# Linear attention with a gated projection on one core: 128-token states, stacked scores, log sums on the matrix engine

## The chip, the cores and the metric

The kernel runs on one core of a Trainium2 chip. A core has five engines that run side by side, each through its own list of instructions: TensorE (PE, matrix products into the PSUM memory), VectorE (DVE), ScalarE (ACT), GpSimd (POOL) and SyncE (SP, which here only issues DMA transfers). The metric is the device time of one launch in microseconds (us).

## The reference

```python
f = 1.0 / (1.0 + np.exp(-f_logit))
state = np.zeros((B, H, D, D))
for t in range(S):
    state = f[:, :, t, :, None] * state + np.einsum('bhd,bhe->bhde', k[:, :, t], v[:, :, t])
    y[:, :, t] = np.einsum('bhd,bhde->bhe', q[:, :, t], state)
x = y.transpose(0, 2, 1, 3).reshape(B, S, H * D)
gate = sigmoid(causal_conv(x, conv_w))        # 5 taps, per channel
out = (gate * (x @ w_val)) @ w_out
```

B = 4, H = 8, S = 768, D = 48, so H * D = 384. Everything is float32. Three weights come as float64 and are turned into float32 on the chip.

## The kernel before, in words

Tokens are cut into NC = 6 chunks of C = 128; each is worked as two halves of HC = 64 tokens. Two heads (s = 0, 1) are stacked on the partitions, at rows 0 and 64, so B * H = 32 heads are BP = 16 pairs; `h` = 0, 1 names a half of the pairs (HP = 8). The recurrence is taken in chunks. For chunk c:

- `pexp`, `pln` (ACT) make log(1 + exp(-f_logit)); `scan` (DVE) sums it along the tokens of a chunk; `exp2` and `exp1` (ACT) make e to the plus and minus that sum; `pmulk`, `pmulq` (DVE) multiply k and q by them.
- `scores` (PE) multiplies k and q inside each half of 64 tokens; `mask` (DVE) copies the product from PSUM to `asb` with the causal triangle `tri`.
- `ktrans` (PE) turns k over, `kevac` (ACT) copies it to `ksb`, `dstate` (PE) makes what each half of 64 tokens adds to the state: u = 0 for the first half, u = 1 for the second. `stmid` (DVE) adds the first to get `mid`, the state in the middle of the chunk, `stend` (DVE) adds the second, and `stmul` (POOL) multiplies by the chunk's whole decay. There is thus a state for each 64 tokens.
- `apply` (PE) sums into x: q on the state (`st` for the first half, `mid` for the second) and `asb` on v. In n = 0 the matmuls use tiles of 64 rows by 32 columns of the array, in n = 1 tiles of 128 by 32.
- `xevac` (ACT) copies x to `xf`. Then the projection of chunk n: `msplit`, `mlow` split x into two float32r parts, `mval` and `mout` are the two products (9 matmuls of 512 columns for each third m of the 384 channels), the convolution is either `conv` (PE, chunks 0, 1, and 5 in two halves named 5 and 6) or `mlast` and `mconv` (ACT and DVE, chunks 2 to 4), then `gate`, `mmul`, `mhigh`, `mrest`, `mstore` and `out`.

The order of all this is the string `PROGRAM`: pieces written out by hand, one after another. `Ordered.call` (line 114, which is the line of nearly every row of the profile) ties each instruction of PE, DVE and ACT to the one before it on its engine, so each engine runs its pieces strictly in that order. `busy n` puts n matmuls on zeros in front of the next piece that takes a PSUM buffer. PSUM has three buffers `pair` and two `mps`: a piece that takes a `pair` waits until the last reader of that buffer is done.

A float32 matmul that is written once is two matmuls in the trace (a half of `scores` is 32 written and 64 in the trace); a transpose is one.

Of the kernel before, what the change touches and what calls it, by code (L numbers as in the profile page):

```python
# [48 lines left out]
loadf 0 0; pexp 0 0; pln 0 0; scan 0 0; loadf 0 1; pexp 0 2; loadk 0 1; wload 0; weight 0; weight 0; weight 0; weight  # L49
0; weight 0; weight 0; pln 0 2; scan 0 2; pexp 0 1; pln 0 1; scan 0 1; loadk 0 2; exp2 0 2; pmulk 0 2; busy 44; ktrans  # L50
0 1; exp1 0 2; loadq 0 2; pmulq 0 2; busy 1; scores 0 1; wload 1; weight 1; weight 1; weight 1; exp2 0 1; pmulk 0 1;
weight 1; mask 0 1; weight 1; exp2 0 0; exp1 0 1; kevac 0 1; exp1 0 0; loadv 0 2; busy 2; dstate 0 1; stmid 0 1; busy
3; apply 0 1 0; apply 0 1 1; loadf 1 0; pexp 1 0; pln 1 0; weight 1; weight 1; weight 1; weight 0; weight 2; halo 0;
stend 0 1; stmul 0 1; loadk 0 0; loadv 0 1; loadq 0 0; pmulk 0 0; loadq 0 1; pmulq 0 0; pmulq 0 1; okc 0; busy 2;
scores 0 0; ktrans 0 0; kevac 0 0; loadv 1 1; scan 1 1; exp2 1 1; exp1 1 1; weight 3; scan 1 0; exp2 1 0; exp1 1 0;
loadk 1 1; loadv 0 0; loadq 1 0; dstate 0 0; stmid 0 0; mask 0 0; apply 0 0 0; apply 0 0 1; stend 0 0; loadk 1 0;
pmulk 1 1; ktrans 1 1; weight 2; weight 3; xevac 0 1; kevac 1 1; loadq 2 1; loadq 1 1; pmulk 1 0; ktrans 1 0; kevac 1
0; dstate 1 1; weight 3; pmulq 1 0; scores 1 0; xevac 0 0; msplit 0; stmul 0 0; loadf 2 0; pexp 2 0; pln 2 0; weight
2; pmulq 1 1; mask 1 0; weight 3; weight 2; busy 1; scores 1 1; mask 1 1; weight 2; stmid 1 1; weight 2; weight 2;
stend 1 1; weight 3; okc 1; conv 0; gate 0 0; gate 0 1; gate 0 2; scan 2 1; loadv 1 0; dstate 1 0; stmid 1 0; scan 2  # L60
0; apply 1 1 0; apply 1 1 1; apply 1 0 0; apply 1 0 1; stend 1 0; weight 3; exp2 2 1; loadk 2 1; wload 2; pmulk 2 1;
ktrans 2 1; stmul 1 1; weight 2; weight 4; weight 4; weight 4; exp1 2 1; exp2 2 0; halo 1; xevac 1 1; stmul 1 0; pmulq
2 1; scores 2 1; weight 3; weight 3; weight 5; kevac 2 1; loadv 2 1; dstate 2 1; loadq 2 0; weight 4; mlow 0; mval 0
0; mval 0 1; mask 2 1; loadk 2 0; pmulk 2 0; ktrans 2 0; xevac 1 0; weight 4; stmid 2 1; apply 2 1 0; mmul 0 0; exp1 2
0; okc 2; pmulq 2 0; stend 2 1; weight 4; loadq 3 1; weight 5; loadk 3 1; loadf 3 0; pexp 3 0; pln 3 0; scan 3 1;
scores 2 0; kevac 2 0; loadv 2 0; dstate 2 0; stmid 2 0; mask 2 0; weight 4; weight 4; weight 6; stend 2 0; weight 5;
weight 6; weight 6; exp2 3 1; pmulk 3 1; weight 6; mval 0 2; exp1 3 1; msplit 1; weight 5; weight 6; weight 5; apply 2
0 0; apply 2 0 1; halo 2; ktrans 3 1; kevac 3 1; xevac 2 0; mmul 0 2; weight 5; weight 6; apply 2 1 1; xevac 2 1; conv
1; mlow 1; pmulq 3 1; mhigh 0 0; mmul 0 1; mrest 0 0; mhigh 0 2; weight 6; weight 5; scan 3 0; loadv 3 0; loadv 3 1;
scores 3 1; mask 3 1; stmul 2 1; dstate 3 1; stmid 3 1; loadk 4 0; stmul 2 0; loadf 4 0; pexp 4 0; pln 4 0; mhigh 0 1;  # L70
mrest 0 2; mrest 0 1; stend 3 1; mval 1 0; apply 3 1 0; gate 1 0; mmul 1 0; mlast 2 0; scan 4 0; mconv 2 0 0; apply 3
1 1; gate 1 1; gate 1 2; exp2 3 0; exp1 3 0; loadk 3 0; pmulk 3 0; loadv 4 0; loadq 3 0; loadk 4 1; loadk 5 1; loadq 4
0; mconv 2 0 1; pmulq 3 0; weight 6; halo 3; weight 5; mout 0 0; mstore 0 0; mout 0 2; mstore 0 2; loadq 5 1; out 0 0;
out 0 2; ktrans 3 0; kevac 3 0; exp2 4 0; mout 0 1; scan 4 1; mhigh 1 0; mrest 1 0; pmulk 4 0; loadv 5 1; mstore 0 1;
out 0 1; exp2 4 1; exp1 4 1; mlast 2 1; dstate 3 0; stmid 3 0; scores 3 0; mask 3 0; mval 1 2; mval 1 1; okc 3; mmul 1
2; mlast 2 2; mhigh 1 2; apply 3 0 0; apply 3 0 1; stend 3 0; mconv 2 1 0; mmul 1 1; mhigh 1 1; mconv 2 0 2; mrest 1
2; mrest 1 1; mout 1 2; msplit 2; xevac 3 1; exp1 4 0; mstore 1 2; xevac 3 0; stmul 3 1; mout 1 1; mstore 1 1; stmul 3
0; loadk 5 0; loadf 5 0; pexp 5 0; out 1 2; mout 1 0; mstore 1 0; out 1 1; loadv 4 1; out 1 0; ktrans 4 0; kevac 4 0;
mconv 2 1 1; pmulk 4 1; ktrans 4 1; mconv 2 1 2; mconv 2 2 0; mconv 2 1 3; pmulq 4 0; scores 4 0; mconv 2 2 1; mconv 2
0 3; mlow 2; mconv 2 2 2; dstate 4 0; mask 4 0; mconv 2 2 3; stmid 4 0; pln 5 0; scan 5 0; mval 2 0; gate 2 0; mmul 2  # L80
0; mval 2 1; gate 2 1; mmul 2 1; scan 5 1; apply 4 0 0; mval 2 2; gate 2 2; mmul 2 2; mhigh 2 1; mrest 2 1; mhigh 2 0;
mrest 2 0; apply 4 0 1; loadv 5 0; kevac 4 1; dstate 4 1; mhigh 2 2; exp2 5 1; exp1 5 1; mrest 2 2; mout 2 0; mstore 2
0; mlast 3 2; mlast 3 0; stend 4 0; loadq 4 1; pmulq 4 1; scores 4 1; mout 2 2; mstore 2 2; pmulk 5 1; stmid 4 1; okc
4; mask 4 1; apply 4 1 0; apply 4 1 1; pmulq 5 1; stend 4 1; mconv 3 0 0; mconv 3 2 0; msplit 3; out 2 0; mconv 3 2 1;
mlow 3; mlast 3 1; mconv 3 1 0; mconv 3 0 1; mconv 3 1 1; mconv 3 0 2; mconv 3 0 3; mconv 3 2 2; ktrans 5 1; kevac 5
1; halo 4; xevac 4 1; mout 2 1; mstore 2 1; mval 3 1; exp2 5 0; exp1 5 0; gate 3 0; xevac 4 0; stmul 4 0; stmul 4 1;
dstate 5 1; stmid 5 1; scores 5 1; mask 5 1; mconv 3 2 3; gate 3 2; mconv 3 1 2; mconv 3 1 3; gate 3 1; mval 3 0; mmul
3 0; mhigh 3 0; apply 5 1 0; apply 5 1 1; halo 5; xevac 5 1; mlast 4 1; loadq 5 0; out 2 2; pmulq 5 0; pmulk 5 0; okc
5; msplit 6; mval 3 2; mmul 3 2; mhigh 3 2; scores 5 0; mmul 3 1; mrest 3 0; mask 5 0; ktrans 5 0; kevac 5 0; mhigh 3
1; conv 6; gate 6 0; mlast 4 2; dstate 5 0; mrest 3 2; mrest 3 1; mout 3 0; mstore 3 0; gate 6 1; gate 6 2; out 2 1;  # L90
mlow 6; stmid 5 0; mval 6 0; mmul 6 0; mconv 4 1 0; mconv 4 1 1; mout 3 2; mhigh 6 0; mrest 6 0; mlast 4 0; mconv 4 0
0; out 3 0; mout 3 1; mstore 3 2; out 3 2; mval 6 2; mstore 3 1; out 3 1; mconv 4 0 1; mconv 4 0 2; mconv 4 1 2; mmul
6 2; mhigh 6 2; msplit 4; mconv 4 0 3; mconv 4 2 0; mrest 6 2; mval 6 1; mmul 6 1; mhigh 6 1; apply 5 0 0; apply 5 0
1; mconv 4 2 1; xevac 5 0; mrest 6 1; mout 6 2; gate 4 0; mstore 6 2; msplit 5; out 6 2; mout 6 0; mstore 6 0; out 6
0; mout 6 1; mstore 6 1; out 6 1; mconv 4 1 3; mlow 4; mval 4 1; mval 4 0; mlow 5; check 0; mval 5 0; mconv 4 2 2;
mmul 4 0; gate 4 1; mmul 4 1; mhigh 4 1; mconv 4 2 3; gate 4 2; mval 5 2; mval 4 2; mmul 4 2; mrest 4 1; mhigh 4 0;
mrest 4 0; mhigh 4 2; mrest 4 2; conv 5; gate 5 0; mmul 5 0; gate 5 1; gate 5 2; mval 5 1; mmul 5 1; mhigh 5 1; mout 4
0; mhigh 5 0; mrest 5 0; mmul 5 2; mrest 5 1; mout 4 2; mstore 4 0; out 4 0; mhigh 5 2; mrest 5 2; mstore 4 2; out 4
# [683 lines left out]
```

## Time and profile before

| what | value |
|---|---|
| median of 3 runs | 231.31 us (230.03, 231.31, 234.48) |
| the profiled execution, its own time | 233.41 us |
| its span in the profile | 231.2 us, so 2.2 us lie around it |
| ScalarE, GpSimd busy | 137.3 us (59%), 42.2 us (18%) |
| weight loads of TensorE busy | 146.0 us (63%) |
| read from and written to HBM | 29.11 MB and 4.72 MB |
| largest loads | `v` 640 KB in 8.7 us, `k` 512 KB in 4.9 us, `q` 512 KB in 6.7 us from issue to landing |

Busy shares are averages over stages with different limits: the first 40 us load at over 370 GB/s, the second half hardly loads. PE counts a matmul as busy while it is in the pipeline, so several overlap. "issue" as the releaser of a wait is time for which the profile shows nothing that the engine waited for.

### The profile page before, as it was taken

What the parts mean: (1) busy time and instruction counts of PE and PEld (TensorE: products, weight loads), DVE (VectorE), ACT (ScalarE), POOL (GpSimd) and SP (SyncE); (2) the same over time, 40 slices, a digit from 0 to 9 for tenths busy, and PEclk for the clock granted to TensorE, in tenths of its full rate; (3) what the DMA queues carried; (4) which work ended last, traced back from release to release, by engine and by line L of the source; (5) the groups of instructions that cost most, each with busy time, mean ns of one, the idle gap of its engine ahead of it and who ended that gap; (6) DMA issues with size and microseconds to landing.
All of it is one profiled execution on the core that took longest, in us unless ns stands there. A gap on an engine that the chain in (4) does not pass through costs nothing.

```text
span 231.2 us, 10393 instructions
## 1 busy us (share of the span) xinstructions
PE 190.3 (82%) x4805; PEld 146.0 (63%) x4809; DVE 165.4 (72%) x204; ACT 137.3 (59%) x198; POOL 42.2 (18%) x52
## 2 busy tenths in 40 slices
...
PEclk9999755575999599979999999999999999999997
...
GB/s 204 371 415 416 421 417 109 239 240 96 6 188 382 118 3 96 234 264 100 94 209 162 110 366 125 3 4 96 45 7 3 3 50 94 48 23 3 45 136 34
DMA packets 10129, 34.56 MB, mean 149 GB/s; under 512 B 1248, under 2 KB 2016, under 8 KB 9184
## 3 DMA queue, kind: packets, MB, share of 16 engines
...
q8 instruction: 39, 0.64, 1.1%
...
HBM read 29.11 MB, written 4.72 MB: 146 GB/s over the span
## 4 chain that ended last, share of the span: by engine, by line
PE 66%; issue 13%; DVE 9%; DMA 5%; ACT 3%; SPq 1%; POOL 0%; DVEq 0%; ACTq 0%; POOLq 0%
PE pair L114 43%; PE mps L114 23%; DMA rawcw<-in_cw 2%; DMA out<-osb 2%; DVE asb L114 2%; DVE pre L114 1%; ACT e L114 1%; DVE e L114 1%; DVE qb L114 1%; DVE mid L114 1%; DVE kb L114 1%; DVE xL L114 1%; ACT ksb L114 1%; DVE rg L114 1%; SPq L648 1%
## 5 line engine op out<-in xcount | busy, mean ns | idle before, releaser
L114 ACT ACTIVATE e<-e 112x1024 f32<-112x1024 f32 (+2 forms) x42 | 48.9, 1179 | 6.1 <-DMA e<-in_f 3.8
L114 PE MATMUL pair<-asb,vb 128*32 128x64 f32 (+1 forms) x1152 | 29.1, 235 | 10.5 <-issue 10.5
L114 DVE TENSOR_TENSOR_SCAN e<-keep,e 112x1024 f32<-112x1024 bf16 (+1 forms) x13 | 29.8, 2301 | 0.3 <-ACT e L114 0.2
L114 PEld LDWEIGHTS pair<-asb,vb 128*32 128x32 f32 (+1 forms) x1152 | 22.6, 117 | 11.3 <-issue 11.3
L366 POOL TENSOR_TENSOR st<-st,e 112x512 f32<-112x512 f32 x10 | 17.1, 1709 | 64.6 <-DVE st L114 37.6
L114 ACT COPY ksb<-pair 128x864 f32<-128x864 f32 x12 | 10.6, 881 | 28.9 <-PE pair L114 28.7
L114 DVE SCALAR_TENSOR_TENSOR pre<-xf,cws,pre 128x512 f32<-128x512 f32 x36 | 26.6, 764 | 0.2
L114 DVE TENSOR_TENSOR asb<-pair,tri 128x1024 f32<-128x1024 f32 x12 | 14.7, 1221 | 15.6 <-PE pair L114 12.7
L114 PE MATMUL pair<-qb,kb 48*64 48x64 f32 x768 | 16.2, 231 | 9.8 <-issue 9.6
L114 PE MATMUL mps<-rg,woH 128*128 128x512 f32 x72 | 23.3, 404 | 0.0
L114 PEld LDWEIGHTS pair<-qb,kb 48*64 48x64 f32 x768 | 14.0, 144 | 13.2 <-issue 12.4
L114 PE MATMUL pair<-qb,mid 48*32 48x64 f32 (+1 forms) x576 | 17.9, 231 | 3.1 <-DVE asb L114 2.0
L114 PE MATMUL pair<-xf,WD 32*32 32x512 f32 (+1 forms) x280 | 19.7, 633 | 0.0
L114 PE MATMUL mps<-xf,WD 32*32 32x256 f32 (+1 forms) x200 | 19.7, 555 | 0.0
L114 PE MATMUL pair<-vb,ksb 64*48 64x64 f32 x704 | 16.5, 243 | 3.2 <-ACT ksb L114 1.9
L114 PEld LDWEIGHTS pair<-vb,ksb 64*48 64x48 f32 x704 | 14.4, 140 | 6.4 <-ACT ksb L114 2.4
L114 DVE TENSOR_TENSOR kb<-kb,e 112x1024 f32<-112x1024 f32 (+1 forms) x13 | 18.3, 1416 | 0.0
L114 PE MATMUL pair<-idle 128*128 128x512 bf16 x49 | 14.7, 455 | 4.2 <-DVE pair L114 3.7
L114 PE MATMUL mps<-xH,wvH 128*128 128x512 f32 x39 | 17.0, 436 | 0.0
L114 PE MATMUL mps<-xL,wvH 128*128 128x512 f32 x39 | 16.2, 416 | 0.3 <-DVE xL L114 0.3
L114 PE MATMUL mps<-xH,wvL 128*128 128x512 f32 x39 | 16.0, 409 | 0.0
L114 DVE TENSOR_TENSOR qb<-qb,e 112x1024 f32<-112x1024 f32 (+1 forms) x13 | 15.8, 1222 | 0.0
(108 smaller groups left out, 380.9 us busy)
## 6 DMA issues: line engine op xcount, KB each, us to landing
...
```

The lines of the kernel that those rows point to most:

```text
L114: ins = emit(*a, **kw)
L366: nc.gpsimd.tensor_tensor(out=s, in0=s, in1=E1[c % NB][:112, HS[h], C - 1 : C].to_broadcast([112, HP, HC]), op=ALU.mult)
L648: nc.sync.dma_start(dst[: src.shape[1]], src[c, :, x0:x1])
```

## The change

**One state per 128 tokens.** `dstate` contracts over all 128 tokens at once, from a second layout of v (`vs`, loaded by the new `loadw`, 512 KB for each half of a chunk's pairs). `stmid` and `mid` are gone, `stend` of chunk 0 takes the decay along with it, and the last chunk makes neither `ktrans` nor `dstate`.

**Scores.** They are made for one batch b of four pairs at a time. Of the four quarters of a 128 by 128 block three are made: the first 64 keys against all 128 queries (a matmul of 128 columns) and the last 64 keys against the last 64 queries. `mask` copies the two triangles, the new `cross` (ACT) the full quarter. `asb` has three buffers in place of two.

**Apply.** n = 0 is now the state alone (tiles of 64 by 32, then 112 by 32), n = 1 the scores alone (64 by 32, then 128 by 32); the first matmuls of each have 128 columns.

**Log sums.** For chunks 0 and 1 f comes with the tokens on the partitions (`ft`), and `csum` (PE) sums with one matmul for each pair against the triangle `below`; `exp1` and `exp2` read the sum from PSUM. The scans of these two chunks are gone.

**Order.** `PROGRAM` is written anew from beginning to end.

```diff
+CUM = (0, 1)
...
+    def csum(c, x0, x1):
+        t = pair("c", c, x0)[:].rearrange("p a t -> p (a t)")
+        for i in range(x1 - x0):
+            PE.matmul(t[:112, i * C : i * C + C], logs(c, x0, x1)[:, i], below[:], start=True, stop=True)
...
     def ktrans(c, h):
+        t = pair("k", c, h)[:].rearrange("p a t -> p (a t)")
+        for i in range(HP):
+            PE.transpose(t[:, i * C : i * C + 112], kb[c % NB][:112, h * HP + i], ident[:112, :112])
...
     def dstate(c, h):
+            for s in range(2):
+                PE.matmul(t[rows(s), 0, i * HC : i * HC + HC], ks[:, i, s], vs[:, h * HP + i, s * HC : s * HC + HC],
+                          start=True, stop=True, tile_position=(0, s * HC))
...
+    def scores(c, b):
+        t, qt, kt = pair("s", c, b), qb[c % NB], kb[c % NB]
+        for p in range(NP):
             for u in range(2):
                 for s in range(2):
+                    at = HC * (s ^ u)
+                    PE.matmul(t[at : at + HC, u, p * C : p * C + C - u * HC], kt[rows(s), b * NP + p, u * HC : u * HC + HC],
+                              qt[rows(s), b * NP + p, u * HC :], start=True, stop=True, tile_position=(s * 64, at))
...
+    def mask(c, b):
+        DVE.tensor_tensor(out=ASB[aslot(c, b)][:, :, 0:HC],
+                          in0=held["s", c, b][:].rearrange("p u (a t) -> p (u a) t", t=C)[:, :, 0:HC],
+                          in1=tri[:].unsqueeze(1).to_broadcast([C, 2 * NP, HC]), op=ALU.mult)
+    def cross(c, b):
+        ACT.copy(ASB[aslot(c, b)][:, 0:NP, HC:], held["s", c, b][:, 0].rearrange("p (a t) -> p a t", t=C)[:, :, HC:])
+        done("s", c, b)
...
     def apply(c, h, n):
+        for b in range(2):
+            for z in range(NP):
+                bp = (2 * h + b) * NP + z
+                for s in range(2):
+                    if n == 0:
+                        lhs, rhs = st[rows(s), bp, 32:64], qt[rows(s), bp]
+                    else:
+                        r = slice(s * HC, s * HC + HC)
+                        lhs, rhs = vt[r, bp, 32:64], ASB[aslot(c, 2 * h + b)][r, z]
...
+                if n == 0:
+                    ops = [(1, 0, st[:, bp, 0:32], qt[:112, bp])]
+                else:
+                    ops = [(1, 0, vt[:, bp, 0:32], at_[:, z])]
+                    ops += [(g, 1, vt[:, bp, VA + at : VA + at + 32], at_[:, NP + z, 0:HC]) for g, at in ((0, 32), (1, 0), (2, 64))]
...
+        "loadw": lambda c, h: load(vs[:, HS[h]], vn, c, h * HP, h * HP + HP),
```

Three places of the new order. The first is PE at the start, before. The rows stand behind the 44 matmuls on zeros (`idle`): the transposes of k (`kb`) for pairs 8 to 15 of chunk 0 come next, then the scores of q (`qb`) and k. Each row says what is written, what is read, and the shape written, with the count of equal ones.

```order
L114 MATMUL pair_100<-idle 128x512
L114 MATMUL pair_100<-ident,kb_66 128x48 x18
L114 LDWEIGHTS idle
L114 MATMUL pair_101<-idle 128x512
L114 MATMUL pair_101<-qb_64,kb_66 64x64 x32
```

The same place after the change (`below` is the triangle, `e_81` the logarithms of f). The sum of pairs 0 to 3 stands directly behind the 44, then come four matmuls on zeros, and the rows begin at the last of these.

```order
L119 MATMUL pair_102<-idle 128x512
L119 MATMUL pair_102<-below,e_81 112x128 x4
L119 MATMUL pair_103<-below,e_81 112x128 x8
L119 LDWEIGHTS idle
L119 MATMUL pair_101<-idle 128x512
L119 MATMUL pair_101<-ident,kb_66 128x112 x8
```

Before, the transposes are the first real work behind the 44; now the sums of all three parts of chunk 0 stand between, and the transposes wait for what is made from the sums.

The second place is PE in the apply of one half of the pairs, before (chunk 2; `st` and `mid` are the states, `asb` the masked scores, `vb` is v).

```order
L114 MATMUL pair_100<-qb_64,st_73 32x64 x8
L114 MATMUL pair_100<-qb_64,mid 32x64 x8
L114 MATMUL pair_100<-asb_84,vb_68 32x64 x8
L114 MATMUL pair_100<-qb_64,st_73 32x64 x8
L114 MATMUL pair_100<-qb_64,mid 32x64 x8
L114 MATMUL pair_100<-asb_84,vb_68 32x64 x8
L114 MATMUL pair_100<-qb_64,st_73 32x64 x4
L114 MATMUL pair_100<-qb_64,mid 32x64 x4
L114 MATMUL pair_100<-asb_84,vb_68 32x64 x16
L114 MATMUL pair_100<-qb_64,st_73 32x64 x4
L114 MATMUL pair_100<-qb_64,mid 32x64 x4
L114 MATMUL pair_100<-asb_84,vb_68 32x64 x16
```

The apply of one half after the change (chunk 1, second half; the transposes of chunk 2 stand in its middle).

```order
L119 MATMUL pair_101<-qb_65,st_75 32x128 x24
L119 MATMUL pair_102<-ident,kb_66 128x112 x8
L119 MATMUL pair_101<-asb_84,vb_69 32x128 x8
L119 MATMUL pair_101<-asb_85,vb_69 32x128 x8
L119 MATMUL pair_101<-asb_84,vb_69 32x128 x4
L119 MATMUL pair_101<-asb_84,vb_69 32x64 x12
L119 MATMUL pair_101<-asb_85,vb_69 32x128 x4
L119 MATMUL pair_101<-asb_85,vb_69 32x64 x12
```

96 written matmuls of 64 columns are now 72, of which 48 have 128 columns.

The third place is ACT, before, from the first copy of turned k (`ksb`) to the second; `e_81`, `e_82` and `e_83` hold the sums and their exponentials, `work` and `wvH` are weights.

```order
L114 COPY ksb_87<-pair_100 128x864
L114 ACTIVATE e_81<-e_81 112x512
L114 ACTIVATE e_82,sums<-e_82 112x2048
L114 ACTIVATE e_82<-e_82 112x2048
L114 CAST wvH<-work 128x384
L114 COPY ksb_86<-pair_102 128x864
```

The same stretch after the change.

```order
L119 COPY ksb_87<-pair_101 128x768
L119 ACTIVATE e_82<-e_82 128x1792
L119 COPY asb_85<-pair_102 128x4x64
L119 ACTIVATE e_83<-pair_103 112x1024
L119 ACTIVATE e_81<-pair_103 112x1024
L119 COPY asb_84<-pair_101 128x4x64
L119 ACTIVATE work<-work 128x384
L119 ACTIVATE e_83<-pair_102 112x1024
L119 COPY ksb_88<-pair_103 128x768
```

The copies of the full quarter (`asb<-pair`) now stand between long exponentials, and the `pair` buffer of the scores comes free only when its copy is done.

More of the change, by code (lines that the diff above doesn't have):

```diff
@@ L48 @@
 PROGRAM = """
[L49 to L98, printed above, removed]
@@ L99 @@
-2; mout 5 0; mout 5 1; mstore 5 0; out 5 0; mstore 5 1; out 5 1; mout 4 1; mstore 4 1; out 4 1; mout 5 2; mstore 5 2;
-check 1; check 2; out 5 2
+loadf 0 0; halo 0; pexp 0 0; pln 0 0; busy 44; csum 0 0; loadf 0 1; pexp 0 1; pexp 0 2; pln 0 1; busy 4; csum 0 1; pln
+0 2; csum 0 2; exp2 0 0; exp2 0 1; exp1 0 0; loadq 0 1; loadk 0 1; pmulk 0 1; loadq 0 0; loadk 0 0; pmulk 0 0; busy 1;
+ktrans 0 0; exp1 0 1; pmulq 0 1; wload 0; weight 0; weight 0; weight 0; weight 0; pmulq 0 0; busy 3; scores 0 1;
@@ new lines @@
+weight 0; mask 0 1; weight 0; weight 0; loadf 1 0; pexp 1 0; loadk 0 2; loadw 0 0; kevac 0 0; dstate 0 0; stend 0 0;
+scores 0 0; mask 0 0; pln 1 0; cross 0 1; csum 1 0; exp2 0 2; exp1 0 2; wload 1; pmulk 0 2; ktrans 0 1; cross 0 0;
+csum 1 1; okc 0; loadq 0 2; pmulq 0 2; weight 1; weight 1; weight 1; weight 1; weight 1; weight 1; exp2 1 0; loadv 0
+0; kevac 0 1; loadw 0 1; dstate 0 1; exp1 1 0; loadv 0 1; apply 0 0 1; stend 0 1; scores 0 3; exp2 1 1; exp1 1 1;
+loadk 1 0; pmulk 1 0; ktrans 1 0; weight 1; xevac 0 0; scores 0 2; kevac 1 0; loadk 1 1; pmulk 1 1; ktrans 1 1; weight
@@ new lines @@
+2; mask 0 3; cross 0 3; loadq 1 0; pmulq 1 0; busy 2; scores 1 0; weight 2; weight 2; weight 1; weight 3; weight 3;
+kevac 1 1; apply 1 0 0; mask 0 2; cross 0 2; scores 1 1; mask 1 0; cross 1 0; loadf 2 0; pexp 2 0; loadv 0 2; apply 0
+1 1; xevac 0 1; weight 2; weight 3; okc 1; weight 2; weight 3; weight 2; weight 3; mask 1 1; cross 1 1; loadq 1 1;
+pmulq 1 1; pln 2 0; weight 3; weight 2; loadw 1 0; dstate 1 0; stend 1 0; scores 1 2; mask 1 2; cross 1 2; msplit 0;
+scan 2 0; exp2 2 0; exp1 2 0; loadw 1 1; dstate 1 1; stend 1 1; scores 1 3; loadv 1 0; apply 1 0 1; halo 1; xevac 1 0;
@@ new lines @@
+conv 0; apply 1 1 0; scan 2 1; exp2 2 1; mask 1 3; weight 3; cross 1 3; mlow 0; wload 2; loadk 2 0; loadk 2 1; pmulk 2
+1; ktrans 2 1; loadv 1 1; apply 1 1 1; weight 2; weight 4; stmul 1 1; stmul 1 0; weight 3; mval 0 1; weight 5; weight
+4; weight 4; exp1 2 1; okc 2; weight 4; gate 0 0; kevac 2 1; weight 4; weight 4; weight 4; pmulk 2 0; ktrans 2 0;
+loadq 2 0; pmulq 2 0; gate 0 1; loadw 2 1; dstate 2 1; weight 5; weight 5; weight 5; gate 0 2; xevac 1 1; mmul 0 1;
+weight 5; scores 2 1; kevac 2 0; stend 2 1; weight 4; weight 6; weight 6; scores 2 0; mask 2 1; weight 5; weight 6;
@@ new lines @@
+mask 2 0; weight 6; loadf 3 0; pexp 3 0; pln 3 0; loadw 2 0; dstate 2 0; stend 2 0; weight 6; weight 6; cross 2 1;
+cross 2 0; mhigh 0 1; weight 5; mval 0 2; apply 2 0 0; loadq 2 1; pmulq 2 1; mval 0 0; msplit 1; scan 3 0; exp2 3 0;
+scores 2 3; mmul 0 0; scores 2 2; mask 2 2; cross 2 2; loadq 3 1; weight 6; scan 3 1; mhigh 0 0; halo 2; stmul 2 1;
+loadv 2 0; loadk 3 0; loadv 2 1; apply 2 0 1; mask 2 3; xevac 2 0; loadw 3 1; stmul 2 0; loadf 4 0; pexp 4 0; cross 2
+3; pmulk 3 0; mrest 0 0; mrest 0 1; mmul 0 2; mlow 1; pln 4 0; scan 4 0; loadk 4 0; loadk 3 1; exp2 3 1; pmulk 3 1;
@@ new lines @@
+conv 1; apply 2 1 0; ktrans 3 0; kevac 3 0; apply 2 1 1; mval 1 1; loadk 4 1; loadq 3 0; loadw 3 0; dstate 3 0; gate 1
+0; gate 1 1; mmul 1 1; ktrans 3 1; mhigh 0 2; mrest 0 2; xevac 2 1; weight 5; weight 6; halo 3; gate 1 2; scan 4 1;
+mval 1 2; mmul 1 2; exp1 3 1; pmulq 3 1; mlast 2 0; mconv 2 0 0; exp1 3 0; mout 0 2; mstore 0 2; exp2 4 0; mout 0 0;
+mstore 0 0; kevac 3 1; pmulq 3 0; pmulk 4 0; mout 0 1; mhigh 1 2; loadv 4 1; loadq 4 1; loadq 4 0; loadv 4 0; out 0 2;
+dstate 3 1; scores 3 2; stend 3 0; mconv 2 0 1; scores 3 3; stend 3 1; stmul 3 1; mstore 0 1; mhigh 1 1; mask 3 2;
@@ new lines @@
+2 2 3; pmulq 4 0; pln 5 0; scan 5 1; kevac 4 0; gate 2 0; gate 2 1; pmulq 4 1; scan 5 0; mval 2 1; mmul 2 1; apply 3 1
+0; ktrans 4 1; loadw 4 1; out 1 2; loadv 3 1; apply 3 1 1; scores 4 1; kevac 4 1; dstate 4 1; xevac 3 1; gate 2 2;
+mhigh 2 1; mlast 3 2; mask 4 1; dstate 4 0; stend 4 0; stend 4 1; mval 2 2; mmul 2 0; mhigh 2 0; okc 4; mmul 2 2;
+cross 4 1; scores 4 0; mask 4 0; cross 4 0; scores 4 2; scores 4 3; mconv 3 2 0; mrest 2 1; mhigh 2 2; mrest 2 2;
+mrest 2 0; out 1 1; loadv 5 1; loadq 5 0; exp2 5 0; exp1 5 0; apply 4 0 0; apply 4 0 1; halo 4; xevac 4 0; mout 2 1;
@@ L305, in gla_moe @@
     rows = lambda s: slice(s * 64, s * 64 + D)
-    held, spare, free, uses = {}, list(pairs), list(mps), [8 * NC + sum(n < NC - 1 for n in CONV)]
+    held, spare, free, uses = {}, list(pairs), list(mps), [10 * NC - 4 + sum(n < NC - 1 for n in CONV) + sum(2 if c else 3 for c in CUM)]
     def pair(*key):
```

215 lines of the change are left out of this document (99 added, 116 removed).

## The prediction

> **What bounds the kernel now.** I read the page first, then busy time by stage, then the chain of waits in a stretch where TensorE (PE) is much idle, then PE's waits and single rows.
>
> ```profile
> span 231.2 us, 10393 instructions
> PE 190.3 (82%) x4805; PEld 146.0 (63%) x4809; DVE 165.4 (72%) x204; ACT 137.3 (59%) x198; POOL 42.2 (18%) x52
> PEclk9999755575999599979999999999999999999997
> ...
> q8 instruction: 39, 0.64, 1.1%
> ```
>
> PE is the busiest, but its granted clock falls to about half in slices 5 to 10 and again in slice 14. The q8 row is the fetching of instructions: 39 packets with 0.64 MB, about 16 KB each. PE's 4805 matmuls and 4809 weight loads are most of the program's instructions, so about 256 of them, or 128 matmuls with their loads, come in one packet.
>
> The stages, cut at the first transposes (16.09 us), at the end of the second convolution on PE (108.43) and at PE's last product; after the stretch, each engine's busy time and count, the granted clock, and the DMA share with GB/s:
>
> ```profile
> 0.00:16.09 16.09, 12.44 (x45) 4.97 (x46) 12.67 (x16) 9.78 (x17) 7.12 (x27) 1.00 0.84 325
> 16.09:108.43 92.34, 66.84 (x2227) 50.06 (x2233) 64.32 (x72) 49.55 (x63) 28.41 (x19) 0.80 0.58 214
> 108.43:224.90 116.47, 110.97 (x2539) 91.00 (x2539) 88.22 (x116) 78.01 (x120) 6.68 (x6) 1.00 0.23 79
> 224.90:231.20 6.30, 0.00 (x0) 0.00 (x0) 0.15 (x1) 0.00 (x0) 0.00 (x0) 0.74 0.19 61
> ```
>
> So the middle stage is bound by no engine (PE 66.84 of 92.34 at clock 0.80), and the late one by PE (110.97 of 116.47). What holds the middle stage is seen in the chain (start, length, what), and in PE's waits of that stage and of the whole run (total, times, longest):
>
> ```profile
> 59.06 1.85 PE pair L114 x118
> 60.91 0.42 issue
> 61.33 2.16 PE pair L114 x128
> 63.49 1.16 issue
> 64.65 1.82 PE pair L114 x103
> 66.47 1.91 issue
> 68.38 2.64 PE pair L114 x126
> 71.02 3.96 issue
> 74.98 2.41 PE pair L114 x43
> ```
> ```profile
> PE pair L114 <- issue: 22.1, 13, 4.0
> ...
> PE pair L114 <- issue: 24.0, 15, 4.0
> PE pair L114 <- ACT ksb L114: 1.9, 2, 1.0
> ```
>
> PE stops after 128 matmuls (61.33), again after about 128, each time for nothing that another engine does. **PE waits for its own instructions**: 22.1 us in 13 waits in the middle stage, 1.9 in the late one.
>
> **The change part by part: how many matmuls.** Scores stay at 64 written for a chunk. The apply goes from 192 to 144 (chunk 0 from 144 to 96), `dstate` from 64 to 32, the transposes from 36 to 16; chunk 5 loses `dstate` (32) and transposes; `csum` adds 32 in all, zeros 5. Float32 counts double, so apply -576, `dstate` -384, transposes -136, `csum` +64, zeros +5: 4805 becomes 3778. From the first transposes to the point where the second convolution and the apply of chunk 2 are done, I count 1696 against the stage's 2227. Both orders reach this point with the same work behind them, but for some of the projection.
>
> **What one matmul costs.**
>
> ```profile
> 159.47 0.35 PE L114 MATMUL pair<-qb,st 48*32 48x64 f32 x16
> ...
> 159.93 0.22 PE L114 MATMUL pair<-asb,vb 64*32 64x64 f32 x1
> 160.29 0.34 PE L114 MATMUL pair<-asb,vb 64*32 64x64 f32 x12
> 160.57 0.32 PE L114 MATMUL pair<-qb,st 112*32 112x64 f32 x8
> 160.81 0.63 PE L114 MATMUL pair<-asb,vb 128*32 128x64 f32 x32
> 162.05 0.76 PE L114 MATMUL pair<-ident,kb 48*128 48x48 f32 x18
> ...
> 17.10 1.16 PE L114 MATMUL pair<-qb,kb 48*64 48x64 f32 x64 [0.25 <-DVE work L114]
> ...
> 18.73 1.11 PE L114 MATMUL pair<-vb,ksb 64*48 64x64 f32 x64
> ```
>
> A run of equal rows lasts one matmul's 0.22 us and the steps between starts: (0.63 - 0.22) / 31 = 13.2 ns in the apply (four tiles of 32 columns), (1.16 - 0.22) / 63 = 14.9 in the scores and (1.11 - 0.22) / 63 = 14.1 in `dstate` (four tiles each). So one tile takes 64 columns every 53 to 60 ns, whether it is loaded with 32, 48 or 64 columns of weights: the streamed columns set it. No row has a float32 matmul of 128 columns on such a tile; it costs between the same 13.2 ns (were it set by the instruction) and 26.4; by the three shapes I take 26.4, 106 ns a tile.
>
> Executed counts times that, for one chunk: scores 64 x 26.4 + 64 x 13.2 = 2.5 us against 128 x 14.9 = 1.9, so **+0.6**. `dstate`: 64 on two tiles at 53 / 2 = 1.7 against 128 x 14.1 = 1.8, **0**. Apply: a half took 2.6 us (from 159.47 to the transposes at 162.05); after, 64 matmuls of 128 columns on eight tiles (0.85), 32 on four (0.85) and 48 of 64 on four (0.64) make 2.3, **-0.2** a half. Transposes: 18 in steps of (0.76 - 0.22) / 17 = 32 ns, 0.6 a half; 8 of 112 columns are 0.4 to 0.8 (half or all of 53 ns for each 64), **0**. Chunk 5 saves 1.8 / 2 + 1.1 = **2.0**. `csum` is 32 executed matmuls a chunk on one undivided tile, by the neighbours 0.8 to 3.4 us; I take **3.4**, as no second tile shares the time.
>
> Changing the tile has a price of its own: the last of the twelve above starts about 0.12 us after 160.29, and the next shape at 160.57, 0.15 us later. The new apply goes through 64 by 32 and 128 by 32 twice instead of once, and scores come in four pieces: some 30 more changes, **+4.5** over the run. [...]
>
> In streamed time PE thus gains nothing: three chunks' scores +1.9, one `csum` +3.4, apply -1.2 and changes of tile +2 make **+6** in the middle stage; +1.9 - 2.0 - 1.2 + 2.5 = **+1** in the late one.
>
> **The start.**
>
> ```profile
> 3.65 12.51 PE L114 MATMUL pair<-idle 128*128 128x512 bf16 x44 [3.65 <-DVE pair L114]
> 16.09 0.76 PE L114 MATMUL pair<-ident,kb 48*128 48x48 f32 x18
> L114 DVE TENSOR_TENSOR_SCAN e<-keep,e 112x1024 f32<-112x1024 bf16 x11 | 27.4, 2500 | 0.1
> L114 DVE TENSOR_TENSOR_SCAN e<-keep,e 112x512 f32<-112x512 bf16 x2 | 2.4, 1209 | 0.2 <-ACT e L114 0.2
> L114 DVE TENSOR_TENSOR kb<-kb,e 112x512 f32<-112x512 f32 x2 | 1.4, 682 | 0.0
> L114 ACT ACTIVATE e<-e 112x512 f32<-112x512 f32 x8 | 4.8, 622 | 2.5 <-DMA e<-in_f 2.4
> ```
>
> The 44 matmuls on zeros end at 16.16, with k ready: the scans of chunk 0 (2 x 1.2 + 2.5 us on DVE) lie under them. Now the same 44 stand ahead of the first `csum`, so the sums begin at 16.2. Then 0.85 of sum, 0.85 of four zeros, 0.85 of the second sum (18.8), about 0.2 to hand over, 0.62 for `exp2` and 2 x 0.68 for `pmulk`: transposes at 21.0, **4.9 us late**. Were k made ready under the zeros as before, this would be 0; the order above does not do that. The scans saved (9.8 us on DVE in both chunks) pay nothing here.
>
> **The other engines.**
>
> ```profile
> L114 DVE TENSOR_TENSOR asb<-pair,tri 128x1024 f32<-128x1024 f32 x12 | 14.7, 1221 | 15.6 <-PE pair L114 12.7 <-ACT xH L114 2.5 <-ACT osb L114 0.4
> L114 DVE TENSOR_TENSOR mid<-st,pair 112x512 f32<-112x512 f32 x12 | 8.2, 683 | 9.6 <-PE pair L114 8.2 <-POOL work L237 1.4
> L114 DVE TENSOR_TENSOR gt<-mps,gt 128x512 f32<-128x512 f32 x13 | 8.8, 684 | 6.3 <-PE mps L114 6.3
> L114 ACT COPY ksb<-pair 128x864 f32<-128x864 f32 x12 | 10.6, 881 | 28.9 <-PE pair L114 28.7
> L114 ACT COPY xf<-pair 128x256 f32<-128x256 f32 x12 | 4.6, 381 | 0.0
> ```
>
> DVE: masks 24 x 0.68 = 16.4 for 14.7, `mid` -8.2, scans -9.8, in all -16. ACT: `cross` 24 x 0.38 = +9.1, two `ksb` fewer and the rest shorter -2.8, in all +6; it has 43 us of room in the middle stage and 38 in the late one, so I cost it at nothing. Without that room it is 6 us. POOL loses two of ten decays, off the path.
>
> **The sum, against the profiled span.** Start: 16.1 + 4.9. Middle stage: 2227 matmuls are 17.4 packets, 92.3 / 17.4 = 5.3 us each; 1696 are 13.2, and if a packet keeps its 5.3 us, because PE streams longer in it but waits less, 70. If only the waits shrink with the count (22.1 x 0.24 = 5.3) and all streaming is added (+6), 93. 13 of 17.4 packets ended in a wait, which is for the first; the clock and the half-full pipeline after a wait are in the other. I take **79**. Late stage: PE's idle 5.5 us there, and some 11 us less DVE work in the two later stages together, against +1 of streaming: between 0 and -7, I take -4, **112.5**. Tail unchanged at 6.3. 16.1 + 4.9 + 79 + 112.5 + 6.3 = 218.8. The run's own time lies 2.2 above its span (233.41), and the median of the runs 2.1 below it (231.31), so I forecast **219 us**.
>
> **Rivals.** (1) *Instructions come no faster for being fewer:* were the waits tied to loads that hold up the fetching and not to the count, the middle stage would take 92.3 + 6 - 5 (some waits fall anyway) = 93 and the late one 114: 231. For it: the wait of 3.96 us lies in slice 13 of the row below, where loads run at 382 GB/s. Against it: 128 matmuls between waits. (2) *Slower, through the PSUM handover:* a `pair` of scores is free only after DVE's mask and ACT's `cross`; behind a late `cross` on ACT stand the next exponentials and the `ksb` copies, for which `dstate` waits, and PE behind it has nothing else to do, its order being fixed. Price: PE's waits for ACT's `ksb` are 0.95 us each; 24 handovers x 0.95 = 23 on top, 242. It makes the kernel 2% slower from 0.7 us a handover on. Against it: ACT is busy 54% in the middle stage, and the short masks and copies free the buffer sooner than one of 1.22 us. (3) *Loads:*
>
> ```profile
> GB/s 204 371 415 416 421 417 109 239 240 96 6 188 382 118 3 96 234 264 100 94 209 162 110 366 125 3 4 96 45 7 3 3 50 94 48 23 3 45 136 34
> ```
>
> ten loads of `vs` with 512 KB are 5 MB more; four of them (2.1 MB) fall into the first 35 us, which run at 415 GB/s already: 5 us later where chunk 1 waits for them, 224 to 225. (4) *Better:* the packet keeps 5.3 us in full and PE's idle time in the late stage goes: 16.1 + 4.9 + 70 + 110 + 6.3 = 207. [...]
>
> **How the numbers follow.** The forecast with 211 to 226 has 0.50, (4) 0.10, (3) 0.10, (1) 0.17 with 227 to 235, (2) 0.13. Range 207 to 235: it takes in half of (4) and all of (1) and (3), and leaves out (2) and the rest of (4), 0.18. Two per cent, about what can be told from no change here, is 226.7 to 235.9: faster 0.50 + 0.10 + 0.06 = 0.66, same 0.04 + 0.17 = 0.21, slower 0.13.
>
> **What would show it.** The first sum at 16.2 and the transposes near 21; some 3780 matmuls; PE's waits for nothing at 10 to 15 us instead of 24.0, still 128 matmuls apart; scores of 128 columns at 26 ns on four tiles; the second convolution ending near 100 us. The forecast is wrong if those waits stay above 20 us, if PE waits more than 10 us in all for ACT, or if matmuls of 128 columns cost no more than those of 64, which would take a further 5 us off.

## The result, and the profile after

The changed kernel takes 218.88 us (median of 4 runs, 218.54 to 219.54) against 232.89 us before (230.03 to 236.23, 4 runs): a ratio of 0.9492, 95% interval 0.9432 to 0.9552. Forecast were 219 us in a range of 207 to 235. A ratio leaves out the executions that a slower state of the chip lengthened, so it is not the quotient of the medians, which are of all. The profiled execution took 218.75 us, 1.75 of them outside its span.

The page: span and instructions, busy time, granted clock, instruction fetching.

```profile
span 217.0 us, 8352 instructions
PE 196.5 (91%) x3776; PEld 151.1 (70%) x3778; DVE 147.7 (68%) x200; ACT 140.1 (65%) x220; POOL 33.4 (15%) x43
PEclk9999999966999999999999999999999999999996
q8 instruction: 31, 0.51, 1.0%
```

PE is busy 6.2 us longer than before (190.3) and idle 20.5 us instead of 40.9. Eight instruction packets fewer come in (31 for 39), and the clock is down in two slices and the last, not in eight and the last.

PE's waits over the whole run (total, times, longest), and where the longest of them stand in the chain of waits:

```profile
PE pair L119 <- issue: 4.4, 3, 2.5
PE pair L119 <- DVE pair L119: 3.6, 1, 3.6
PE pair L119 <- ACT osb L119: 2.0, 2, 1.3
...
PE pair L119 <- ACT xf L119: 1.0, 1, 1.0
...
PE pair L119 <- ACT asb L119: 0.3, 1, 0.3
```
```profile
33.15 1.13 issue
...
43.72 2.51 issue
...
65.20 0.75 issue
```

The waits for nothing fell from 24.0 us in 15 waits to 4.4 in 3. The new handover through `cross` shows 0.3 us (`asb`), and no wait for ACT's `ksb` is left, so the rival of the PSUM handover is refuted.

The stages, cut at the same marks as before (first transposes; second convolution and apply of chunk 2 done; last product):

```profile
0.00:20.04 20.04, 16.29 (x80) 8.98 (x81) 5.36 (x10) 8.01 (x16) 3.15 (x18) 1.00 0.91 337
20.04:92.38 72.34, 65.56 (x1704) 50.04 (x1705) 59.48 (x75) 53.35 (x75) 25.02 (x18) 0.95 0.79 295
92.38:210.75 118.37, 114.63 (x1994) 92.08 (x1993) 82.87 (x117) 78.74 (x131) 5.26 (x7) 1.00 0.27 91
210.75:217.00 6.25, 0.00 (x0) 0.00 (x0) 0.00 (x0) 0.00 (x0) 0.00 (x0) 0.66 0.23 76
```

| stage | before | forecast | after | off by |
|---|---|---|---|---|
| start | 16.1 | 21.0 | 20.0 | -1.0 |
| middle | 92.3 | 79 | 72.3 | -6.7 |
| late | 116.5 | 112.5 | 118.4 | +5.9 |
| tail | 6.3 | 6.3 | 6.3 | 0 |
| span | 231.2 | 218.8 | 217.0 | -1.8 |

The total is so close because two errors cancel, and that is luck. The late stage, forecast shorter, became longer, and the reason stands in PE's rows of chunk 4 at full clock (start, length, what, count):

```profile
126.57 1.24 PE L119 MATMUL pair<-qb,st 48*32 48x128 f32 x48
127.74 0.99 PE L119 MATMUL pair<-ident,kb 112*128 112x112 f32 x8
128.65 1.91 PE L119 MATMUL pair<-asb,vb 64*32 64x128 f32 x96
130.50 1.09 PE L119 MATMUL pair<-qb,kb 48*64 48x128 f32 x32
131.52 1.99 PE L119 MATMUL pair<-vs,ksb 128*48 128x64 f32 x64
...
135.73 2.84 PE L119 MATMUL pair<-qb,kb 48*64 48x128 f32 x96
...
138.50 1.24 PE L119 MATMUL pair<-qb,st 48*32 48x128 f32 x48
```

From start to start, a quarter of the scores (32 matmuls) takes 131.52 - 130.50 = 1.02 us, and three in a row (138.50 - 135.73) / 3 = 0.92 each, where 0.64 was forecast; a half of the apply takes 1.17 + 1.85 = 3.0 where 2.3 and the changes of tile were, and 2.6 before; transposes take 0.91 with the change of tile. Only `dstate` came as forecast (64 in 1.99).

### The profile page after: what moved, and what is told of

It reads as the page before. It is cut to its first block, busy times and chain, and to the rows that moved or that the text cites. A ratio compares the mean times of both kernels' runs of the same rounds, so it can differ in the third digit from the quotient of the medians.

```text
span 217.0 us, 8352 instructions
## 1 busy us (share of the span) xinstructions
PE 196.5 (91%) x3776; PEld 151.1 (70%) x3778; DVE 147.7 (68%) x200; ACT 140.1 (65%) x220; POOL 33.4 (15%) x43
## 4 chain that ended last, share of the span: by engine, by line
PE 87%; DVE 3%; issue 3%; ACT 2%; DMA 1%; DVEq 0%; ACTq 0%
PE pair L119 60%; PE mps L119 27%; DMA out<-osb 1%; ACT osb L119 1%; DVE keep L119 0%; DVE pair L119 0%; ACT xf L119 0%; DVE e L119 0%; DVE kb L119 0%; ACT qb L119 0%; DVE asb L119 0%; DVE st L119 0%; DVE pre L119 0%; DVE gt L119 0%; ACT e L119 0%
## 5 line engine op out<-in xcount | busy, mean ns | idle before, releaser
L119 ACT ACTIVATE e<-e 112x1024 f32<-112x1024 f32 (+4 forms) x32 | 39.7, 1247 | 4.2 <-DMA e<-in_ft 1.9
L119 PE MATMUL pair<-asb,vb 128*32 128x64 f32 (+2 forms) x1152 | 24.4, 252 | 4.4 <-issue 4.4
L119 PE MATMUL pair<-qb,kb 48*64 48x64 f32 (+1 forms) x768 | 25.0, 260 | 1.3 <-DVE st L119 0.9
L119 DVE TENSOR_TENSOR kb<-kb,e 112x1024 f32<-112x1024 f32 (+1 forms) x13 | 16.4, 1272 | 12.9 <-ACT e L119 12.9
L119 DVE TENSOR_TENSOR asb<-pair,tri 128x512 f32<-128x512 f32 x24 | 16.4, 686 | 12.5 <-PE pair L119 12.5
L119 PEld LDWEIGHTS pair<-qb,kb 48*64 48x64 f32 x768 | 21.3, 136 | 4.6 <-DVE st L119 1.0
L119 DVE TENSOR_TENSOR_SCAN e<-keep,e 112x1024 f32<-112x1024 bf16 x8 | 19.1, 2385 | 1.3 <-issue 1.3
L119 ACT COPY xf<-pair 128x512 f32<-128x512 f32 (+1 forms) x24 | 10.3, 483 | 11.1 <-PE pair L119 11.1
L119 PE MATMUL mps<-xH,wvH 128*128 128x512 f32 x39 | 16.4, 421 | 0.0
L119 ACT ACTIVATE e<-pair 112x1024 f32<-112x1024 f32 (+2 forms) x13 | 9.2, 750 | 11.0 <-PE pair L119 11.0
L119 PE MATMUL pair<-rg,woH 128*128 128x512 f32 (+1 forms) x48 | 12.8, 355 | 2.0 <-ACT osb L119 2.0
L119 ACT COPY asb<-pair 128x256 f32<-128x256 f32 x24 | 8.6, 374 | 8.3 <-DVE asb L119 8.1
```

What stands on the lines that cost most here:

```text
L119: ins = emit(*a, **kw)
```

## The experiments

Theory: PE's instructions come in packets of about 128 matmuls (39 packets for 4805 before, 31 for 3776 after), and where many short matmuls stand together PE outruns them; fewer and longer matmuls take these waits away. Rivals: the waits went with the new order, the other loads or the shorter DVE chain; and the start, put later by the change, costs its 4 us in the end. All times stand beside 218.88 us for the change.

### The count of matmuls put back

First run, in both loops of `apply` (shown for the first):

```diff
-                    PE.matmul(to(b, 2 * s, 0, z), lhs, rhs, start=..., stop=False, ...)
+                    for i in range(2):
+                        w = slice(i * HC, i * HC + HC)
+                        PE.matmul(to(b, 2 * s, 0, z)[:, w], lhs, rhs[:, w], start=(i == 0 and ...), stop=False, ...)
```

> Each float32 matmul of 128 columns in the apply is written as two of 64, so the streamed columns, the order, the loads and the work of the other engines stay as they are after the change, and the executed matmuls on PE rise from 3776 to some 4830, about as many as before it (4805). Theory of supply (PE's instructions arrive in packets of 256 and hold PE up in the middle stage): the waits for nothing return to 15 to 22 us from 4.4, the granted clock falls again in more slices, and the time rises by 8 to 18 us, to 227-237. Rival (the waits went because of the new order, the other loads or the shorter DVE chain, not because of the count): the waits stay at 4 to 7 us and the time within 1.5 us of 218.9.

Measured: 248.63 us (244.68 to 250.65), slower than before the change and above the 227 to 237 expected. Waits for nothing 17.0 us in 12 waits, but PE's busy time rose too, to 208.4 us. The granted clock was 0.990 in the profiled execution, above the changed kernel's 0.975, so the loss is not the clock's. I put the busy time down to the two halves that follow each other on one tile, and the second run wrote them eight tiles apart:

```diff
-        for b in range(2):
+        for b, i in ((b, i) for b in range(2) for i in range(2)):
+            w = slice(i * HC, i * HC + HC)
             for z in range(NP):
...
-                    ops = [(1, 0, st[:, bp, 0:32], qt[:112, bp])]
+                    ops = [(1, i, st[:, bp, 0:32], qt[:112, bp, i * HC : i * HC + HC]) for i in range(2)]
```

> As the first run, but the two halves of 64 columns of an apply matmul are written eight tiles apart and not one behind the other, so that a tile isn't fed twice in a row. In the first run PE's busy time rose by 12 us beside 12.6 us of added waits for nothing. Theory of supply (PE's instructions come too slowly where many short matmuls stand together): about the same 4830 executed matmuls, waits for nothing at 13 to 20 us again, and PE's busy time back to within 3 us of 196.5, so 230 to 238 us. Rival (the first run was slow because the halves hit one tile in a row, and its waits came of that): waits under 8 us and 219 to 223.

Measured: 247.51 us (242.75 to 250.01), ratio to before 1.0496 (1.0374 to 1.0618). From its page, its waits, two links of its chain, and one state part of the apply, its first 64 matmuls (up to 144.50) and the whole:

```profile
span 241.0 us, 10464 instructions
PE 207.9 (86%) x4832; PEld 163.3 (68%) x4834; DVE 148.8 (62%) x200; ACT 140.2 (58%) x220; POOL 32.3 (13%) x43
GB/s 210 398 394 421 425 413 390 173 262 203 177 279 122 241 275 142 74 186 100 121 218 320 158 87 113 91 5 45 93 5 4 5 3 68 112 0 0 68 102 64
q8 instruction: 40, 0.66, 1.1%
```
```profile
PE pair L119 <- issue: 16.4, 13, 2.9
```
```profile
159.30 1.37 issue
172.53 1.47 issue
```
```profile
143.85 0.86 PE L119 MATMUL pair<-qb,st 48*32 48x64 f32 x64
```
```profile
143.85 1.44 PE L119 MATMUL pair<-qb,st 48*32 48x64 f32 x96
```

With 4832 matmuls the packets are 40 and the waits are back, 16.4 us in 13, while the order of the pieces, the loads, DVE and ACT stayed (148.8 and 140.2 us busy against 147.7 and 140.1). That settles the waits: they follow the count and not the order, the loads or the DVE chain. They aren't tied to the loads either: the wait at 159.30 stands in slice 27 of the GB/s row, at 5 GB/s, the one at 172.53 in slice 29, at 93.

The packets can be seen too, as each one on q8 has its time in the trace. Of 76 waits for nothing of over 0.3 us in the 13 profiles, 74 end 1.2 to 1.6 us after a packet has landed. The wait of 2.51 us in the changed kernel, for one, ends at 46.23, and a packet ran from 43.93 to 45.01. Before and after the change no two packets start less than 3.3 us apart (3.34 and 3.44 at the least). The 128 short matmuls at 61.33 before the change were done in 2.16 us; 128 of the new scores take about 3.7 (four quarters of 0.92). So here the short ones outrun the packets and the long ones do not.

The size was not as expected: the time is above the 230 to 238 forecast, and busy time did not come back to 196.5 but stayed 11.4 us above it, so the halves on one tile were not the reason. From the start of each row to the start of the next, the apply takes 8.7 of these 11.4 us; most of the rest lies in the scores and the projection, at a granted clock of 0.954 for 0.975. For the apply, the last rows say why. These 96 matmuls stream the same columns as the 48 of the changed kernel at 126.57 and take 1.44 us for 1.24. The first 64 of them start (0.86 - 0.22) / 63 = 10.2 ns apart, although 64 columns on eight tiles would be 53 / 8 = 6.6. So here a matmul with its weight load took PE some 10 ns from start to start, more than its columns on eight tiles, and a matmul fewer can save part of that as well as its share of a packet. Of the 24.0 us by which this span is longer, 12.0 are waits and 11.4 busy time. Putting the count back thus costs more than the 14 us that the change brought, about half of it in waits; with it, the new kernel is slower than the old.

### The added loads

```diff
-        "loadw": lambda c, h: load(vs[:, HS[h]], vn, c, h * HP, h * HP + HP),
+        "loadw": lambda c, h: load(vs[:, HS[h]], vn, c, h * HP, h * HP + HP) if c == 0 else None,
```

> The second layout of the values (vs) is loaded for chunk 0 alone: eight loads of 512 KB, 4.2 MB, are left out, and the states of chunks 1 to 4 are made from chunk 0's values. Instructions on PE, DVE and ACT are unchanged. Theory of load cost (rival 3 of the prediction: the added bytes are paid for at some 415 GB/s where chunk 1 waits): 2 to 6 us faster, 213-217. Mine: the loads lie beside other work and only their instruction fetching neighbours feel them: within 1.5 us of 218.9, the waits for nothing at most 1 us shorter.

Measured: 217.56 us (216.35 to 218.04), 1.3 us less; the waits for nothing 3.1 us. The 4.2 MB cost about 1 us at most and not 5, and 1 us is less than these runs can tell apart (see the last of them): the rival of the loads was at best small.

### The start

Two runs bring the first transposes forward. One gives chunk 0 its scans back:

```diff
-CUM = (0, 1)
+CUM = (1,)
-pexp 0 0; pln 0 0; busy 44; csum 0 0; ... busy 4; csum 0 1; ... csum 0 2; ... busy 1; ktrans 0 0;
+pexp 0 0; pln 0 0; scan 0 0; ... scan 0 1; ... scan 0 2; ... busy 44; ktrans 0 0;
```

> The log sums of chunk 0 go back to the scans on DVE, under the 44 matmuls on zeros, which stand directly ahead of the first transposes again; chunk 1 keeps the sums on TensorE. Theory that the start term was real (the sums on PE stand behind the zeros and the transposes come 4 us later for it): transposes at 16.1 instead of 20.0, and the time 3 to 4 us shorter, 215-216. Rival (the start is bound by the loads of k, v and q that follow, or by PE's instruction supply right behind it): the transposes come earlier but the middle stage ends within 1 us of 92.4, time 218-219.5.

The other shortens the zeros:

```diff
-pexp 0 0; pln 0 0; busy 44; csum 0 0;
+pexp 0 0; pln 0 0; busy 20; csum 0 0;
```

> 20 instead of 44 matmuls on zeros ahead of the first sum on TensorE; the logs are ready at 8.2 us. Theory that the zeros alone hold the start up: the sums begin at 8.5 to 10 us instead of 15.3, the transposes at 13.5 to 15 (then bound by the loads of k) and the time 4 to 6 us shorter, 213-215. Rival (loads bind what follows, as in the other run on the start): 217 or more. Rival (the granted clock, with fewer zeros, falls in the first 20 us): PEclk below 9 in the first four slices and the time 219 or more.

Measured: 220.11 us (219.56 to 220.6) and 220.45 us (220.05 to 223.74), so no gain, if anything a loss of 1 us, where 215 to 216 and 213 to 215 were expected if the later start had a cost. The first transposes came 5 us earlier in both; PE's rows of the run with scans in chunk 0, the same marks of the changed kernel, and the links of the chain of that run between them:

```profile
15.03 0.93 PE L119 MATMUL pair<-ident,kb 112*128 112x112 f32 x8
...
76.42 1.96 PE L119 MATMUL pair<-qb,kb 48*64 48x128 f32 x64
...
87.51 1.24 PE L119 MATMUL pair<-qb,st 48*32 48x128 f32 x48
```
```profile
20.04 0.99 PE L119 MATMUL pair<-ident,kb 112*128 112x112 f32 x8
...
79.42 1.96 PE L119 MATMUL pair<-qb,kb 48*64 48x128 f32 x64
...
88.38 1.24 PE L119 MATMUL pair<-qb,st 48*32 48x128 f32 x48
```
```profile
28.59 13.79 DMA e<-in_f
...
54.10 1.00 issue
81.24 1.84 issue
```

A lead of 5.0 us at the transposes is 3.0 at 76.42 and 0.9 at 87.51. The first part goes to the load of chunk 2's f, which ends at 42.4 and holds ACT up, with the copy to `xf` behind it; the second to a wait for nothing of 1.84 us at 81.24, which the changed kernel does not have. The packet that ends this wait ran from 80.86 to 81.82; the one in the same place of the changed kernel, from 79.10 to 80.40, came in time. Why it started later, with PE ahead, is open. (With 20 zeros the same wait stands at 83.23, with 1.80 us.) In all, the waits for nothing are 7.3 and 7.9 us in these two runs, against 4.4. So the start term was right as a row and wrong as a cost: about 4 us of later transposes cost the end nothing.

### The tiles of the scores

In the scores the matmuls of 128 columns always fall on the same two of four tiles. This run swaps the tiles for every second pair of heads in chunk 0 (with the slots in `asb` and the layout of `v` to match):

```diff
-                    at = HC * (s ^ u)
-                    PE.matmul(t[at : at + HC, u, p * C : p * C + C - u * HC], kt[...],
+                    x, y = (p % 2, 2 * u + p // 2) if c == 0 else (0, p)
+                    at = HC * (s ^ u ^ x)
+                    PE.matmul(t[at : at + HC, u ^ x, y * C : y * C + C - u * HC], kt[...],
```

> In the scores of chunk 0 the two tile assignments are swapped for every second pair of heads, so that the matmuls of 128 columns fall on all four tiles in turn instead of always on the same two; the values of chunk 0 are laid out to match. Theory that the imbalance makes a quarter 1.0 us where 0.64 was forecast (16 matmuls of 128 columns on two tiles are 8 x 109 ns; on four tiles 4 x 109 + 4 x 53): chunk 0's four quarters take 0.7 to 0.85 us each in the rows, the others stay at 1.0 to 1.1. Rival (a 128-column matmul costs 32 ns whatever the tile): all stay at 1.0. The time changes by under 1.5 us in either case, since what is won in chunk 0 stands ahead of the waits for nothing.

Measured: 218.99 us (217.27 to 219.98). A swapped quarter of chunk 0, what follows it, and one of chunk 1, unswapped:

```profile
33.87 0.90 PE L119 MATMUL pair<-qb,kb 48*64 48x128 f32 x32
34.70 0.99 PE L119 MATMUL pair<-ident,kb 112*128 112x112 f32 x8
...
37.92 1.09 PE L119 MATMUL pair<-qb,kb 48*64 48x128 f32 x32
```

From 1.02 us (34.59 to 35.61 in the changed kernel) to 34.70 - 33.87 = 0.83. The imbalance is half of what the forecast lacked. With even tiles the columns alone are, by the steps of the prediction, 16 x 26.4 + 16 x 13.2 = 0.64; the other 0.19 is an upper estimate for the change of tile. (In chunk 4 above, a quarter with a change behind it took 1.02 and three in a row 0.92 each, so the change 0.1 to 0.2.) The time does not move, as expected.

### The late stage, the sums, and all together

Three output buffers:

```diff
-    osb = [... for i in range(2)]
+    osb = [... for i in range(3)]
```

> Three output buffers instead of two. PE waits 2.0 us in the late stage for ACT's copies into osb, the first of them behind an output transfer that still reads the buffer. Theory that the late stage is bound by PE and each of its waits is paid: the 2.0 us go to under 0.7 and the time falls by 1 to 2 us, to 217-218. Rival (DVE's chain behind it waits in the same place): the wait goes, the time stays within 0.7 us of 218.9.

Measured: 218.62 us (217.2 to 218.95). PE's wait for `osb` went from 2.0 to 1.4 us and the time by 0.3: less than expected, as what is left of the wait is ACT's copy and not the transfer.

Scans in both chunks, as in the run on the start, with `CUM = ()` and `scan 1 0`, `scan 1 1`:

> The log sums of both chunks 0 and 1 are scans on DVE again (64 executed matmuls fewer on PE, 7 us of its streaming; some 10 us more on DVE), the 44 zeros directly ahead of the first transposes; the rest stays as changed. Theory that the middle stage is set by the loads and by PE's instruction supply and not by streaming: 218 to 222, like the run that undid it for chunk 0 alone. Rival (PE's streaming sets it): 212 to 215. Rival (DVE sets it, and the sums on PE were what relieved it): 224 or more.

Measured: 217.13 us (216.01 to 218.5), 1.8 us less than with the sums on PE.

```profile
PE 192.7 (89%) x3707; PEld 146.7 (68%) x3709; DVE 156.3 (72%) x205; ACT 141.4 (65%) x220; POOL 33.0 (15%) x43
```
```profile
PE pair L119 <- DVE kb L119: 4.2, 1, 4.2
...
PE pair L119 <- ACT xf L119: 1.6, 1, 1.6
```

PE wins 3.8 us of busy time and waits 4.2 for DVE's `kb` behind the scan. The sums it no longer makes took 7.3 us from start to start; part of that goes to the clock, 0.956 for 0.975. None of the three theories fits quite; the nearest is that streaming does not set the stage. The sums on TensorE bring nothing here.

That run had ACT waiting for f of chunk 2. Holding back the load of the output weights:

```diff
+        if n == 2:
+            DVE.memset(RAW[key][0:1, 0, 0:1], 0)
         nc.sync.dma_start(RAW[key][:].rearrange("p n w -> p (n w)"), src)
```

with `wload 2` moved behind `xevac 0 1`.

> The run with scans in both chunks, and the load of the output weights (1152 KB, issued near 21 us there, not needed before some 60 us) held back until x of chunk 0's second half is copied, by a one-element write in front of it (one more DVE instruction). In the run with scans ACT waited 4.60 us for chunk 2's f until 42.12, with the copy to xf, for which PE waited 1.6 us, behind it. Theory that the loads set the first 45 us once the start is earlier: f of chunk 2 lands 2 to 3 us earlier, PE's wait for xf goes and the time falls 1 to 2 us, to 215-216. Rival (PE's instruction supply takes back what is won ahead of 60 us, as in the two runs on the start): the wait for xf goes, the waits for nothing grow, time within 0.8 us of 217.1.

Measured: 218.75 us (215.24 to 219.65). ACT's exponential of that f, with the scans alone and then with the weights held back:

```profile
42.12 1.91 ACT L119 ACTIVATE e<-e 112x2048 f32<-112x2048 f32 x1 [4.60 <-DMA e<-in_f]
```
```profile
39.24 1.91 ACT L119 ACTIVATE e<-e 112x2048 f32<-112x2048 f32 x1 [1.78 <-DMA e<-in_f]
```

The load lands 2.9 us earlier, as meant, and PE's wait for `xf` goes from 1.6 to 1.0 us. The profiled execution took 215.24 us at a granted clock of 0.970, the other four 218.0 to 219.65 at 0.952 to 0.959, so the median shows no gain; why the clock differs between them is open.

Scans, held back weights, three buffers and swapped tiles together, and the changed kernel once more on the same chip:

> The scans in both chunks, the output weights held back, three output buffers and the swapped tiles of chunk 0 together. If each saves what it saved or promised alone (against 218.9: 1.8, 1 to 2, 0.3 and 0 us): 214.5 to 216.5. If PE's waits take back what is won early: 217 to 218.

> The changed kernel itself once more, to stand beside the run with everything together on the same chip: 218.5 to 219.6. A difference between its two sets of runs of more than 0.7 us would say that differences of that size between the other runs tell nothing.

Measured: 217.35 us (216.23 to 220.35, ratio to before 0.931, 0.9252 to 0.9368) and 219.08 us (217.75 to 220.1, 0.940, 0.9349 to 0.9451). Together they give 1.7 us less in the median, with intervals that overlap: perhaps 0.8% better, not shown, and not the 214.5 to 216.5 expected if the single gains added up. The changed kernel's own two medians differ by 0.2 us, while its two ratios differ by 0.9%, so between these variants only more than about 2 us would count. None of the variants that were to make the kernel faster reaches that.

## Why the prediction was right

The cause was right and so was the direction; that the number came out within 0.2 us was luck, by the errors of two stages.

**Waits for instructions: right, and larger than taken.** The step was 22.1 us of waits in the middle stage, falling with 2227 matmuls to 1696 (1704 in fact). The stage took 72.3 us, near the 70 that the prediction had by 5.3 us for each packet and did not take. But 5.3 us is no constant: 72.3 us / (1704 / 128) is 5.4, the two runs with the count put back have 4.9 and 5.0 in the same stage, and the two on the start 5.7 and 5.9. I expected 10 to 15 us of waits; 4.4 are left. The waits do not fall in proportion: they come only where PE is through a packet before the next has landed (74 of the 76 above end 1.2 to 1.6 us after a landing). The second convolution ended near 88, not 100.

**Streaming in the middle stage: too low.** Forecast were +6 us. At 0.92 to 1.02 us a quarter, a chunk's scores take 3.7 to 4.1 us, up to +2 against 1.9 before and not +0.6; a half of the apply +0.4 and not -0.2; `csum` came near the forecast, 16 matmuls in 1.91 us:

```profile
28.48 1.91 PE L119 MATMUL pair<-below,e 128*112 128x128 f32 x16
```

That makes 3.8 us a chunk, for 3.4. With three chunks of scores, six halves and one chunk of sums the stage gets up to 6 + 2.4 + 3.8, some 12 us at full clock. PE's busy time in the stage nevertheless fell, from 66.8 to 65.6 us, and its idle time from 25.5 to 6.8. What hides the 12 us is mostly the clock, which the prediction named and did not price: it rose from 0.80 to 0.95 in this stage, as the waits went. The convolution's matmuls are the same before (the lines with L114) and after, here over the whole run:

```profile
L114 PE MATMUL pair<-xf,WD 32*32 32x512 f32 (+1 forms) x280 | 19.7, 633 | 0.0
L114 PE MATMUL mps<-xf,WD 32*32 32x256 f32 (+1 forms) x200 | 19.7, 555 | 0.0
...
L119 PE MATMUL mps<-xf,WD 32*32 32x256 f32 (+1 forms) x200 | 16.3, 465 | 0.0
...
L119 PE MATMUL pair<-xf,WD 32*32 32x512 f32 (+1 forms) x280 | 15.6, 501 | 0.0
```

The mean of one falls from 633 to 501 and from 555 to 465 ns; with the rest of the projection in the stage that is 5 us less, start to start (22.4 to 17.4). `dstate`, with half the matmuls, gives 2 more.

**The late stage: the failed step.** It was forecast at 112.5 and took 118.4. The term "scores +1.9" was three chunks at 0.6; start to start, the stage's scores went from 6.3 to 11.2 us, +4.9, so 3 of the 5.9 us. The sum spread 16 matmuls of 128 columns over four tiles; the code gives them to two, 8 x 106 ns each, and I did not look at which tile each went to. The apply went from 16.1 to 18.1 us, its changes of tile included, +2.0 where -1.2 and +2.5 stood: 0.7 us more. And PE's idle time fell from 5.5 to 3.7 us, where the forecast took 5 us off: another 3.2. `dstate` and the transposes save 2.9 us where 2.0 was forecast, which gives about 1 back. The wrong term with a cause is thus the scores, taken as if all four tiles shared them.

**Changes of tile** were put at 0.15 us; the rows give 0.1 to 0.2, an estimate.

**The start** was right in the row (21.0 forecast, 20.0 seen, as the first sum began at 15.25) and wrong in the sum: the runs that took it away won nothing.

**Rivals.** Waits tied to loads: refuted by waits at 5 GB/s. Handover: 0.3 us. Loads: at most about 1 us of 5. The better case of 207 was near in the middle stage (70 for 72.3) and wrong in the late one (110 for 118.4).
